# A rank-32 product in four column groups instead of one zero-padded matmul chain

## The chip, the cores and the metric

The kernel runs on one core of one Trainium2 chip. TensorE (PE, with its weight loads PEld), VectorE (DVE), ScalarE (ACT), GpSimd (POOL) and the queue of SyncE (SP) work side by side and wait for each other by semaphores. The metric is the time of one execution on the device in microseconds; a profile of another execution shows where it goes.

## The reference

Windowed attention with eight global keys, then a mixer over the tokens of low rank (32) and a feed-forward part. B = 4 batches, H = 8 heads, S = 768 tokens, D = 64, so 512 channels; U is 768 x 32, V is 32 x 768, w_ch1 is 512 x 2048, w_ch2 is 2048 x 512.

```python
scores = scale * np.matmul(q, k.transpose(0, 1, 3, 2))
...
scores = np.where(keep, scores + bias, -1e9)
a = softmax(scores)
x = np.matmul(a, v)            # (B, H, S, D), then (B, S, H * D)
...
xt = x.transpose(0, 2, 1)
h = xt @ U @ V
u = x + h.transpose(0, 2, 1)
ch = np.maximum(u @ w_ch1, 0.0) @ w_ch2
return u + ch
```

## The kernel before

**Tiling.** Tokens lie on partitions in NSB = 6 tiles of P = 128. Heads go in pairs (NP = 4 pairs a batch), so one step of the outer loop, `i`, is one pair of one batch: 16 steps. A pair is 128 channels, the chunk `dc`. Scores are made transposed, only for the diagonal and the next block of each key tile (`st_SE`, `st_S`, L352 and L357); after the exponential (`ep`), the product with v (`st_V`, L407 and L411) leaves 128 tokens x 65 columns in `ob`, the last column being the sum to divide by. DVE divides into `x_sb` (L424), POOL casts that to `x16` (L425).

**The mixer.** `st_M1` (L428 to L437) multiplies with U: six matmuls, one per token tile, add into one PSUM tile `tmp_ps`, with `u16[:, n]` as the weights (128 tokens x 128 columns) and `x16` (128 tokens x 128 channels) as the moving input. Only R = 32 columns of `u16` hold U, the other 96 are zeros from a memset (L178), so 96 rows of the result are zero. DVE copies it to `tmp16` (L437, 128 x 128, fp16). The product with V contracts over all 128 partitions of `tmp16` and `v16w`, of whose rows only the first 32 hold V and the others zeros. It is done by `st_M2` (L444) for batch 0, where also x is added by matmuls with an identity (L449); by L511 for batch 0's second copy at the output; and by `st_M3` (L474) for the other batches, whose result DVE adds to `x_sb` (L479). All matmuls of the kernel are thus full: 128 rows and 128 columns of weights.

**Feed-forward.** `mk_up` (L497) makes a 128 x 384 piece of the hidden layer from four matmuls into `hps`; ACT takes it to `htr` with Relu (L501). `mk_down` (L517) adds sixteen hidden chunks into `cps`, DVE adds x (L523), SP stores it. These pieces are queued by `queue_ff` and let out a few at a time by `fill(n)` between the steps of the attention.

**Order.** The whole program is recorded in an order written out by hand (`tc.manual_schedule()`), so each engine takes its instructions in the order of the calls. For batch 0 `st_M1(i - 2)` stands before `st_V(i - 1, 0)`; the last of the four stands right before its `st_M2`. In the later loop `st_M1(i - 1)` comes after `fill(1)` and before `st_E(i, 0)`, and `fill(2)` stands between it and `st_M3(i - 1)`, which needs its `tmp16`.

**Queues.** SP issues the loads of q, k and v; POOL issues those of U, V (L179, L180) and of the weights (L219, L222), and after U and V its next work is the cast of v (L126). `tmp_ps`, `ups`, `hps` and `tp` share three PSUM buffers (tag `th`).

Of the kernel before, what the change touches and what calls it, by code (L numbers as in the profile page):

```python
# [12 lines left out]
FP16 = mybir.dt.float16  # L13
# [7 lines left out]
def kernel(  # L21
# [13 lines left out]
    nc = tc.nc  # L35
    B, H, S, D = q.shape
    NG = int(n_global)
    NL = int(n_local)
    P = 128
    DM = H * D  # L40
    NSB = S // P
# [3 lines left out]
    R = moe_U.shape[1]  # L45
    NP = H // 2
    NPE = 2 * NP
    qk_scale = 1.0 / math.sqrt(D)
    BIG = -1.0e9


    assert NG <= 32 and NL <= P - 32 and NG + NL <= P and D == 64 and S % P == 0

    slope = [2.0 ** (-8.0 * (h + 1) / H) for h in range(H)]

# [8 lines left out]
    cst = ctx.enter_context(tc.tile_pool(name="cst", bufs=1))  # L64
# [18 lines left out]
    def ps_th(name, dtype=FP32, cols=512):  # L83
        return psum.tile([P, cols], dtype, name=name, tag="th", bufs=3)
# [5 lines left out]
    def load_qk(i):  # L90
        b, h0 = i // NP, 2 * (i % NP)
        got = []
        for src, nm in ((q, "qst"), (k, "kst")):
            st = stp.tile([P, 2, NSB, D], FP32, name=nm, tag=nm, bufs=2)
            if i < NPE:
                nc.sync.dma_start(
# [53 lines left out]
    def warm(n):  # L150
# [19 lines left out]
    qz = [  # L170
        [cst.tile([P, S], FP16, name=f"qz{s}_{hi}") for hi in range(2)] for s in range(2)
    ]
    nc.vector.memset(qz[0][0][D:P], 0.0)
    nc.vector.memset(qz[0][1][0:D], 0.0)
    u16 = cst.tile([P, NSB, P], FP16, name="u16")
    v16w = cst.tile([P, S], FP16, name="v16w")
    for t in (qz[1][0][D:P], qz[1][1][0:D], u16.rearrange("p n c -> p (n c)"), v16w):
        nc.gpsimd.memset(t.bitcast(I32), 0)  # L178
    nc.gpsimd.dma_start(u16[:, :, 0:R], moe_U.rearrange("(c p) r -> p c r", p=P))  # L179
    nc.gpsimd.dma_start(v16w[0:R], moe_V)  # L180
    ident16 = cst.tile([P, P], FP16, name="ident16")
    nc.vector.tensor_copy(ident16, ident)

# [41 lines left out]
    xs, x16s, tmps, uTs = {}, {}, {}, {}  # L225
# [59 lines left out]
    def st_A(i):  # L285
        vt = vts[i]
        vA = vap.tile([P, NSB - 1, 2, D + 1], FP16, name="vA", tag="vA")
        if i < NPE:
            nc.gpsimd.tensor_copy(vA, vt[:, 0:NSB - 1])
# [11 lines left out]
    def st_P(i):  # L301
        nc.vector.tensor_copy(
            vas[i][0:NG, 1:].rearrange("p n h d -> p n (h d)"),
            vts[i][0:NG, 0:1].rearrange("p n h d -> p n (h d)").broadcast_to(
                (NG, NSB - 2, 2 * (D + 1))
            ),
        )
# [3 lines left out]
    def turn(i):  # L311
        stq, stk = cast.pop(i)
        qT = kp.tile([P, NSB, P], FP16, name="qT", tag="qT")
        kT = kp.tile([P, S], FP16, name="kT", tag="kT")
        nc.sync.dma_start_transpose(
            kT.rearrange("d (n p) -> d n p", n=NSB), stk.rearrange("p n h d -> p (n h d)")
        )
        nc.sync.dma_start_transpose(qT, stq.rearrange("p n h d -> p (n h d)"))
        turned[i] = qT
        kts[i] = kT  # L320
# [7 lines left out]
    def st_K(i):  # L328
        kT = kts[i]
        kA = kp.tile([P, NSB - 1, P], FP16, name="kA", tag="kA")  # L330
        nc.vector.tensor_copy(kA.rearrange("d n p -> d (n p)"), kT[:, 0:S - P])
        nc.vector.tensor_copy(
            kA[:, 1:, 0:NG], kT[:, 0:NG].unsqueeze(1).broadcast_to((P, NSB - 2, NG))
        )
        kas[i] = kA
# [53 lines left out]
    def st_S(i, c):  # L389
        for hi in range(2):  # L390
            s_dve(i, hi, s_pe(i, hi, c))

    def st_E(i, hi):
        ep = scp.tile([P, W], FP16, name=f"ep{hi}", tag=f"ep{hi}")
        nc.scalar.activation(  # L395
            ep, sps.pop((i, hi)), AF.Exp, scale=slope[2 * (i % NP) + hi]
        )
        eps[i, hi] = ep

    def st_V(i, hi):  # L400
        b, h = i // NP, 2 * (i % NP) + hi
        ep, vt, vA = eps.pop((i, hi)), vts[i], vas[i]
        obf = ps_cps("ob") if (i, hi) == (NP - 1, 1) else ps_ob()
        ob = obf[:, 0:NSB * (D + 1)].rearrange("p (n d) -> p n d", n=NSB)
        for qi in range(NSB):
            if qi:
                nc.tensor.matmul(  # L407
                    ob[:, qi], ep[:, OF[qi - 1]:OF[qi - 1] + P], vA[:, qi - 1, hi],
                    start=True, stop=False,
                )  # L410
            nc.tensor.matmul(  # L411
                ob[:, qi], ep[:, DG[qi]:DG[qi] + P], vt[:, qi, hi],
                start=(qi == 0), stop=True,
            )
        rcp = vap.tile([P, NSB], FP32, name="rcp", tag="rcp")
        nc.vector.reciprocal(rcp, ob[:, :, D])
        xo = xs[b][:, :, h * D:(h + 1) * D]
        x16 = x16s[b][:, i % NP, :, hi * D:(hi + 1) * D]
        rb = rcp.unsqueeze(2).broadcast_to((P, NSB, D))
        if i == NP - 1:  # L420
            nc.vector.tensor_tensor(x16, ob[:, :, 0:D], rb, ALU.mult)
            later.append((xo, ob[:, :, 0:D], rb))
            return
        nc.vector.tensor_tensor(xo, ob[:, :, 0:D], rb, ALU.mult)  # L424
        nc.gpsimd.tensor_copy(x16, xo)  # L425


    def st_M1(i):  # L428
        b, dc = i // NP, i % NP
        ch = slice(dc * P, (dc + 1) * P)  # L430
        tps = ps_th("tmp_ps")
        for n in range(NSB):
            nc.tensor.matmul(  # L433
                tps[:, 0:P], u16[:, n], x16s[b][:, dc, n],
                start=(n == 0), stop=(n == NSB - 1),
            )
        nc.vector.tensor_copy(tmps[b][:, ch], tps[:, 0:P])  # L437

# [147 lines left out]
    for i in range(NP):  # L586
        st_SE(i, 0)
        cast_v(i)
        st_A(i)
        if i < 2:  # L590
            load_v(i + 2)
        if i in (1, 2):
            load_qk(NP - 1 + i)
        if i == 2:
            load_w1(0, 2)
        if i == 3:
            load_v(NP)
        if i >= 2:
            st_M1(i - 2)
        if i:  # L600
            st_V(i - 1, 0)
        st_T(i + 1)
        st_SE(i, 1)
        if i:
            st_V(i - 1, 1)
        st_P(i)
        if i >= 2:
            st_M2(i - 2)
        if i < 3:
            cast_qk(i + 2, nc.gpsimd)  # L610
        if i == 3:
            load_w1(2)
            load_w1(3)
        st_SE(i, 2)
    st_M1(NP - 2)
    st_V(NP - 1, 0)
    st_V(NP - 1, 1)
    cast_qk(NP + 1, nc.gpsimd)
    finish_table()
    st_M2(NP - 2)  # L620
    first = [s_pe(NP, hi, 0) for hi in range(2)]
    st_M1(NP - 1)
    st_M2(NP - 1)
    for xo, o, rb in later:
# [6 lines left out]
    for i in range(NP, NPAIR + 2):  # L631
        b, hp = divmod(i, NP)
        live = i < NPAIR
        n = 1 if i < 2 * NP + 1 else 2
# [14 lines left out]
        if NP < i <= NPAIR:  # L649
            st_V(i - 1, 0)  # L650
        if i + 1 < NPE:
            st_T(i + 1)
# [20 lines left out]
        if live:  # L673
            st_S(i, 2)
            if i < NPE:
                st_P(i)
        if i + 1 < NPAIR:
            if i + 1 >= NPE:
                st_K(i + 1)
# [15 lines left out]
        if live:  # L695
            st_E(i, 1)
        if i + 2 < NPAIR and i + 2 >= NPE:
            turn(i + 2)
# [39 lines left out]
```

## Time and profile before

| What | Value |
|---|---|
| Median of 3 runs | 246.03 us (245.66 to 247.09) |
| Profiled execution, first to last instruction | 243.4 us |
| POOL: memset of u16, of v16w | 0.41 us each, at 3.77 and 4.13 us |
| POOL: issue of the load of U, of V | 1.00 and 0.53 us, at 4.49 and 5.48 us |
| U and V, from issue to landing | 6.1 and 5.4 us |
| L433, first and last start | 17.6 and 182.4 us |

The profile gives starts and lengths in microseconds from the first instruction. A line names the source line, the engine, the operation, the tiles as output<-inputs and their sizes; `128*128` is the part of the array that a matmul uses. Matmuls overlap in the pipeline, and their ends are modelled, so the time that a matmul costs the stream is read from start to start. Idle time stands in brackets with what ended it.

### The profile page before, as it was taken

To read this page: it belongs to the slowest core of one execution; us is meant where nothing else is said; L and a number is where in the kernel's file an instruction comes from. 1 tells how busy PE (TensorE), PEld (TensorE's weight loads), DVE (VectorE), ACT (ScalarE), POOL (GpSimd) and SP (SyncE) were. 2 spreads that over 40 slices of the span, in tenths; PEclk is the share of its full clock that TensorE was granted. 3 is DMA by queue.
4 is the path that set the end of the run, shared out by engine and by line. 5 is a ranking of instruction groups with operands and counts; after the bars stand their busy time and mean duration, and the time that the engine had idled before them with its cause. 6 is when DMAs were issued, how large, how long until landed. Compare 5 with 4: busy or idle time off the path is not lost.

```text
span 243.4 us, 4881 instructions
## 1 busy us (share of the span) xinstructions
PE 230.9 (95%) x1952; PEld 141.7 (58%) x1952; DVE 132.4 (54%) x273; ACT 118.8 (49%) x203; POOL 92.8 (38%) x140
## 2 busy tenths in 40 slices
PE   7899879989999999999999999999999999999994
PEld 2577755656565556675656555666565455555453
DVE  7768964868676967675757666755432111011121
ACT  5898648775822211866462507483733134543300
POOL 8379828474464535453544436332111000000000
PEclk9999999999999999999999999999999999999999
DMA  6999999999387999895958682722121200110022
GB/s 195 319 292 298 223 240 274 198 228 225 83 183 176 210 241 166 239 189 136 213 149 196 167 209 80 166 70 57 46 78 32 87 13 34 43 43 34 12 86 86
DMA packets 86030, 36.61 MB, mean 150 GB/s; under 512 B 74136, under 2 KB 82552, under 8 KB 86008
## 3 DMA queue, kind: packets, MB, share of 16 engines
q1 hardware_dynamic: 81480, 32.01, 52.0%
q0 software_dynamic: 4528, 4.29, 10.9%
q8 instruction: 15, 0.25, 0.4%
q14 instruction: 7, 0.06, 0.1%
HBM read 27.46 MB, written 6.29 MB: 139 GB/s over the span
## 4 chain that ended last, share of the span: by engine, by line
PE 75%; DMA 8%; ACT 6%; DVE 5%; POOL 2%; issue 2%; SPq 0%; POOLq 0%
PE cps L517 33%; PE hps L497 29%; DMA w<-in_moe_w_ch_dram 5%; ACT ep L395 3%; PE sc L352 3%; ACT htr L501 3%; DMA vst<-in_v_dram 2%; PE sc L357 2%; PE ob L411 2%; PE cps L535 1%; PE ob L407 1%; PE tmp_ps L433 1%; DVE sp L383 1%; PE ups L474 1%; DVE qz L282 1%
## 5 line engine op out<-in xcount | busy, mean ns | idle before, releaser
L501 ACT ACTIVATE htr<-hps 128x384 f16<-128x384 f32 x128 | 61.7, 491 | 89.6 <-PE hps L497 88.5
L497 PE MATMUL hps<-uT,w 128*128 128x384 f16 x512 | 97.9, 326 | 2.2 <-DMA w<-in_moe_w_ch_dram 1.0
L517 PE MATMUL cps<-w,htr 128*128 128x512 f16 x368 | 90.7, 379 | 0.0
L497 PEld LDWEIGHTS <-w 128*128 128x128 f16 x512 | 47.8, 98 | 33.7 <-issue 2.3
L383 DVE SCALAR_TENSOR_TENSOR sp<-sc,relcat 128x512 f32<-128x512 f32 (+1 forms) x72 | 43.1, 640 | 26.5 <-PE sc L357 21.6
L517 PEld LDWEIGHTS <-htr 128*128 128x128 f16 x368 | 34.6, 98 | 32.6
L523 DVE TENSOR_TENSOR osb<-cps,x_sb 128x512 f32<-128x512 f32 x23 | 15.9, 690 | 51.2 <-PE cps L517 50.9
L395 ACT ACTIVATE ep<-sp 128x1408 f16<-128x1408 f32 x24 | 32.7, 1372 | 12.4 <-DVE sp L383 12.4
L425 POOL CAST x<-x_sb 128x384 f16<-128x384 f32 x30 | 15.4, 513 | 60.4 <-DVE x_sb L424 60.4
L352 PE MATMUL sc<-qz,kT 128*128 128x128 f16 x192 | 27.6, 219 | 0.5 <-DVE sp L383 0.5
L357 PE MATMUL sc<-qz,kA 128*128 128x128 f16 x160 | 25.3, 219 | 0.2 <-DVE kA L276 0.2
L352 PEld LDWEIGHTS <-kT 128*128 128x128 f16 x192 | 18.3, 98 | 4.2 <-DVE kT L261 0.4
L357 PEld LDWEIGHTS <-kA 128*128 128x128 f16 x160 | 15.6, 98 | 6.8 <-issue 0.8
L482 POOL CAST x<-x_sb 128x768 f16<-128x768 f32 x12 | 9.9, 829 | 20.5 <-DVE x_sb L479 20.5
L424 DVE TENSOR_TENSOR x_sb<-ob,rcp 128x384 f32<-128x384 f32 x30 | 16.7, 557 | 1.0
L479 DVE TENSOR_TENSOR x_sb<-ups,x_sb 128x384 f32<-128x384 f32 x24 | 12.3, 552 | 7.7 <-PE ups L474 7.6
L411 PE MATMUL ob<-v,ep 128*128 128x65 f16 x192 | 15.8, 193 | 0.0
L126 POOL CAST v<-vst 128x768 f16<-128x768 f32 x16 | 13.4, 840 | 4.6 <-DMA vst<-in_v_dram 4.6
L411 PEld LDWEIGHTS <-ep 128*128 128x128 f16 x192 | 13.9, 98 | 2.1
L407 PE MATMUL ob<-vA,ep 128*128 128x65 f16 x160 | 13.9, 194 | 0.0
L326 POOL COPY qz<-qT 64x768 f16<-64x768 f16 x16 | 13.4, 836 | 0.7 <-DMA qT<-q 0.2
L407 PEld LDWEIGHTS <-ep 128*128 128x128 f16 x160 | 10.9, 97 | 2.1
(79 smaller groups left out, 196.7 us busy)
## 6 DMA issues: line engine op xcount, KB each, us to landing
qst<-in_q_dram SPq DMA_DIRECT2D x16, 384.0 KB, 5.4
kst<-in_k_dram SPq DMA_DIRECT2D x16, 384.0 KB, 5.2
vst<-in_v_dram SPq DMA_DIRECT2D x16, 384.0 KB, 6.3
out_dram<-osb SPq DMA_DIRECT2D x23, 256.0 KB, 2.0
w<-in_moe_w_ch_dram POOLq DMA_DIRECT2D x6, 512.0 KB, 8.7
vA<-v SPq DMA_DIRECT2D x8, 152.3 KB, 3.6
w<-in_moe_w_ch_dram POOLq DMA_DIRECT2D x1, 1024.0 KB, 12.4
out_dram<-osb SPq DMA_DIRECT2D x2, 128.0 KB, 1.7
```

The source lines that it names most:

```text
L352: nc.tensor.matmul(sc[:, o:o + P], kT[:, kb * P:(kb + 1) * P], z[:, kb * P:(kb + 1) * P], start=(o == 0 and not on_pe), stop=(o + P == tot),)
L357: nc.tensor.matmul(sc[:, o + P:o + 2 * P], kA[:, kb], z[:, (kb + 1) * P:(kb + 2) * P], start=False, stop=(o + 2 * P == tot),)
L383: nc.vector.scalar_tensor_tensor(out=sps[i, hi][:, c0:c0 + tot], in0=sc[:, 0:tot], scalar=qk_scale / slope[2 * (i % NP) + hi], in1=relf[:, ...
L395: nc.scalar.activation(ep, sps.pop((i, hi)), AF.Exp, scale=slope[2 * (i % NP) + hi])
L407: nc.tensor.matmul(ob[:, qi], ep[:, OF[qi - 1]:OF[qi - 1] + P], vA[:, qi - 1, hi], start=True, stop=False,)
L411: nc.tensor.matmul(ob[:, qi], ep[:, DG[qi]:DG[qi] + P], vt[:, qi, hi], start=(qi == 0), stop=True,)
L424: nc.vector.tensor_tensor(xo, ob[:, :, 0:D], rb, ALU.mult)
L425: nc.gpsimd.tensor_copy(x16, xo)
L497: nc.tensor.matmul(hps[:, 0:GT], w1_16[:, dc, jt * P:(jt + 1) * P], uT[:, dc, ts], start=(dc == 0), stop=(dc == NDC - 1),)
L501: nc.scalar.activation(cell["htr"][:, jt], hps[:, 0:GT], AF.Relu)
L517: nc.tensor.matmul(cps, htr[:, jc, t * P:(t + 1) * P], w2_16[:, jc], start=(b > 0 and jc == 0), stop=(jc == NJC - 1),)
L523: nc.vector.tensor_tensor(osb, cps, x_sb[:, n], ALU.add)
```

## The change

Each of the six matmuls with U now uses 32 columns of weights and writes to its own group of 32 PSUM partitions: token tile n goes to group g = n % 4, so groups 0 and 1 get two token tiles, groups 2 and 3 one. `tmp_ps` then holds four partial sums one above the other. V is loaded four times, one copy per group of 32 partitions of `v16w`, so that the product with V, which contracts over 128 partitions as before, adds the four partial sums. `u16` shrinks to its 32 columns, and its memset and that of `v16w` go.

```diff
+    NG4 = P // R
...
-    u16 = cst.tile([P, NSB, P], FP16, name="u16")
+    u16 = cst.tile([P, NSB, R], FP16, name="u16")
     v16w = cst.tile([P, S], FP16, name="v16w")
-    for t in (qz[1][0][D:P], qz[1][1][0:D], u16.rearrange("p n c -> p (n c)"), v16w):
+    for t in (qz[1][0][D:P], qz[1][1][0:D]):
         nc.gpsimd.memset(t.bitcast(I32), 0)
-    nc.gpsimd.dma_start(u16[:, :, 0:R], moe_U.rearrange("(c p) r -> p c r", p=P))
-    nc.gpsimd.dma_start(v16w[0:R], moe_V)
+    nc.gpsimd.dma_start(u16, moe_U.rearrange("(c p) r -> p c r", p=P))
+    for g in range(P // R):
+        nc.gpsimd.dma_start(v16w[g * R:(g + 1) * R], moe_V)
...
         for n in range(NSB):
+            g = n % NG4
             nc.tensor.matmul(
-                tps[:, 0:P], u16[:, n], x16s[b][:, dc, n],
-                start=(n == 0), stop=(n == NSB - 1),
+                tps[g * R:(g + 1) * R, 0:P], u16[:, n], x16s[b][:, dc, n],
+                start=(n < NG4), stop=(n + NG4 >= NSB),
             )
```

The order of the instructions on every engine stays as it was, but for the two memsets and the three loads on POOL. The first weight load with `tmp16` waits for all loads of V, and three of the later loads of weights on POOL wait for loads of U and V that were issued long before.

More of the change, by code (lines that the diff above doesn't have):

```diff
@@ L52 @@
     assert NG <= 32 and NL <= P - 32 and NG + NL <= P and D == 64 and S % P == 0
+    assert R == 32
     slope = [2.0 ** (-8.0 * (h + 1) / H) for h in range(H)]
```

## The prediction

> **What bounds the kernel now.** I read the page first, then a table of stretches, then PE's waits, then the matmuls around the edited product one by one. One profiled execution is the base: 243.4 us from first to last instruction. The median of the runs shown is 246.03, so 2.6 us lie around the span; every term below is added to both alike.
>
> ```profile
> PE 230.9 (95%) x1952; PEld 141.7 (58%) x1952; DVE 132.4 (54%) x273; ACT 118.8 (49%) x203; POOL 92.8 (38%) x140
> ...
> PEclk9999999999999999999999999999999999999999
> ```
>
> PE is busy 95% at a full granted clock. That average hides three stages, which the table of stretches separates (after the stretch and its length: PE, PEld, DVE, ACT and POOL busy, then clock, DMA share and GB/s).
>
> ```profile
> 0.00:33.10 33.10, 27.53 (x334) 19.23 (x334) 25.23 (x67) 24.54 (x47) 23.71 (x42) 1.00 1.04 267
> 33.10:64.00 30.90, 28.50 (x276) 19.40 (x277) 21.81 (x41) 22.49 (x38) 17.88 (x27) 1.00 1.15 219
> 64.00:184.50 120.50, 119.27 (x1038) 73.08 (x1036) 77.32 (x155) 54.55 (x84) 50.39 (x70) 1.00 0.63 151
> ```
>
> Up to 33.1 the DMA engines are full (share 1.04) and PE has gaps; from 64 to 184.5 PE is busy 119.27 of 120.50, and anything that PE does longer there makes the kernel longer. PE's waits from 64 us to the end are only these:
>
> ```profile
> PE ups L474 <- DVE tmp L437: 0.6, 2, 0.4
> PE ups L474 <- ACT htr L501: 0.4, 1, 0.4
> ```
>
> The early stage ends on a transfer: in the chain that ended last stand a load of v and then the first w_ch1 load, for which PE waits.
>
> ```profile
> 8.04 6.04 DMA vst<-in_v_dram
> ...
> 20.65 12.43 DMA w<-in_moe_w_ch_dram
> ```
>
> ```profile
> 33.13 0.34 PE L497 MATMUL hps<-uT,w 128*128 128x384 f16 x1 [1.03 <-DMA w<-in_moe_w_ch_dram]
> ```
>
> **The product with U, and what a switch can cost.** L433 runs 16 times with six matmuls each. Its matmuls (least, median and greatest ns), then, from the timeline of PE, one of its turns in the full stream (start us, length us, engine, line, operation):
>
> ```profile
> L433 PE MATMUL tmp_ps<-x,u x96: 216/219/219, 17.6 to 182.4; 128*128 128x128 f16 x96
> ```
>
> ```profile
> 132.85 0.81 PE L497 MATMUL hps<-uT,w 128*128 128x384 f16 x4
> 133.50 0.50 PE L433 MATMUL tmp_ps<-x,u 128*128 128x128 f16 x6
> 133.84 0.38 PE L517 MATMUL cps<-w,htr 128*128 128x512 f16 x1
> ```
>
> A matmul lasts 219 ns in the records, but six span 0.50 us: five steps of (498 - 219) / 5 = 56 ns. From 133.50 to the next product at 133.84 is 0.34 us = 6 x 56. That is all that this product costs PE: 16 x 0.334 = 5.3 us. The difference of 219 - 56 = 163 ns is the tail of a matmul that the next one overlaps (for the 384-column form it is 326 less its step of 162, again about 163).
>
> The edit makes each of these a 128 x 32 tile of the array instead of a full one; every other matmul of the program stays 128*128. So PE changes its tile shape 32 times, where before it never did. No row shows a matmul on part of the columns or a change of shape. I bound three pieces.
>
> (a) *Inside the six.* Highest: they keep the 56 ns step, gain nothing. Lowest: the four groups run fully together, so that only one full step lies between the first four and the last two, 4 x 56 = 222 ns gained. The nearest row is the quickest pace at which the trace shows PE starting matmuls, the 65-column ones:
>
> ```profile
> 18.00 0.20 PE L407 MATMUL ob<-vA,ep 128*128 128x65 f16 x1
> 18.04 0.19 PE L411 MATMUL ob<-v,ep 128*128 128x65 f16 x1
> 18.07 0.19 PE L407 MATMUL ob<-vA,ep 128*128 128x65 f16 x1
> ```
>
> About 28 ns a start with one weight load each. I take that pace: 5 x (56 - 28) = 140, rounded down to 138 ns gained.
>
> (b) *Each switch.* Lowest: 0, the stream goes on. Highest: the whole tail is waited for and then a whole weight load of 98 ns (the length of every PEld row of L433) lies open: 163 + 98 = 261 ns. What an open load costs, one row shows: a load that waits with its matmul.
>
> ```profile
> 12.80 0.10 PEld L357 LDWEIGHTS <-kA 128*128 128x128 f16 x1 [0.32 <-DVE kA L276]
> 12.80 0.23 PE L357 MATMUL sc<-qz,kA 128*128 128x128 f16 x1 [0.15 <-DVE kA L276]
> 12.82 0.10 PEld L347 LDWEIGHTS <-slI 128*128 128x128 bf16 x1
> 12.87 0.38 PE L347 MATMUL sc<-rel,slI 128*128 128x512 bf16 x1
> ```
>
> The next start comes 70 ns after, not 56: 14 ns. I take the full tail plus this, 163 + 14 = 177 ns, on the reading that the array is not given another shape while a matmul is in it. [...]
>
> (c) *A full-stream turn:* two switches less the gain, 2 x 177 - 138 = +216 ns (bounds: -222, and 2 x 261 = +522).
>
> **Where it lands.** The 16 turns fall into four groups.
> - Turns 1 to 4 (17.6 to 30.4 us): PE waits 1.03 us at 33.13 for the w_ch1 load, whose issue at 20.65 depends on no turn but for what precedes turn 1. They cost 0; without that cover they would cost 0.04 to 0.2 us each, 0.5 us at most.
> - Turns 5 and 6 (50.11, 61.34): PE stands idle before them (0.54 us for ACT, 0.29 us for POOL), so the entry is free: 177 - 138 = +39 ns each, 0.08 us.
> - Turns at 96.66, 108.47 and 158.61: within 2 us after them PE waits for tmp of DVE or htr of ACT (the rows above, 0.6 + 0.4 us, besides the tail). DVE reaches tmp late because of its copies to kA ahead of it, not because of the product, so 0 each; with the cover gone 216 each, 0.65 us.
> - The other seven, from 71.88 to 182.14: 7 x 0.216 = +1.51 us.
>
> PE together: +1.59 us.
>
> The rest of the edit: DVE's copy of tmp stays 128 x 128, the product with V has the same shapes, PE does the same count of instructions. On POOL two memsets of 0.41 us go and three more loads of V come at 0.53 us of issue each: +0.77 us, in the 4.13 us for which POOL then waits for v:
>
> ```profile
> 10.14 0.83 POOL L126 CAST v<-vst 128x768 f16<-128x768 f32 x1 [4.13 <-DMA vst<-in_v_dram]
> ```
>
> Behind them in POOL's queue stands that cast; were the cover gone, it would be 0.77 us late and the w_ch1 issue with it. The first product with V comes at 20.8 us and the landing of V was at 10.9 (issued at 5.48, 5.4 us to landing), so its wait for four loads is free, as are the waits on these loads that the changed program puts before w_ch issues after 20.65.
>
> But the transfers themselves are not free. The page's queue of POOL's loads:
>
> ```profile
> q0 software_dynamic: 4528, 4.29, 10.9%
> ```
>
> 10.9% of 243.4 us is 26.5 us of all 16 engines for 4.29 MB, thus 0.30 us for one load of V (48.0 KB in the list of DMA issues) and 0.9 us for three. DMA is full there, and v's landing at 14.08 leads the chain to 33.13. Bounds 0 (gaps between packets take it) and 0.9; a gain is excluded, since nothing on that chain waits for the memsets. I take the middle, 0.5 us.
>
> Sum: 1.59 + 0.5 = +2.1 us: span 245.5, **time 248.1 us** (+0.9%). Its own range: least, switches of 163 ns and the 222 ns gain, 7 x 0.104 - 2 x 0.06 + 0 = +0.6 (246.6); most, switches of 261 with 138 gained, 7 x 0.384 + 2 x 0.123 + 0.9 = +3.8 (249.8).
>
> [...]
>
> **The rivals.**
> 1. *The groups overlap and the switches cost nothing* (faster). Each full-stream turn gains 222 ns: 7 x 0.222 + 2 x 0.222 = 2.0 us, less 0.5 for V: 244.5; 244.0 if the loads are hidden. For it: four separate column groups with four separate inputs need nothing of each other. Against: a load and a matmul of another shape would have to run beside a tail of 163 ns. It decides below 2 x 69 ns of switch per turn, where the 138 ns are not yet eaten. 0.2.
> 2. *The groups do not overlap and the switches are short, or the two cancel* (the change does not do what it says). PE +0, V +0.5: 246.5. For it: the pace of 28 ns is of short inputs, and 128 columns took 56 everywhere. 0.15.
> 3. *No overlap, and each switch costs a tail and a whole load* (slower still): 7 x 0.522 + 2 x 0.261 = 4.2, plus 0.9: 251.1. Turns with cover stay covered (522 ns against waits of about as much). Against: the one open load seen cost 14 ns, not 98. 0.15.
>
> **How the numbers follow.** The forecast gets 0.5, the rivals 0.2, 0.15 and 0.15. About 0.5% (1.2 us, so 244.8 and 247.3) is what the runs can tell from no change. Faster: rival 1, 0.2. Same: rival 2 and the lower part of the forecast's range, 0.15 + 0.1 = 0.25. Slower: 0.4 + 0.15 = 0.55. The range runs from just under rival 1 with its loads half hidden, 244.2, to rival 3, 251.0; about 0.1 is left out on each side.
>
> **What will show it.** In the changed profile, at a full-stream turn: the first of the six starts about 177 ns later after the 384- or 512-column step than before (162 or 216 ns), the six starts lie about 28 ns apart, the next matmul starts some 233 ns after the last instead of 56. Starts within a few ns and no gaps at the ends: rival 1. Steps of 56: rival 2 or 3. For V: the cast of v at 14.13 and the hps start at 33.13 move by up to 0.9 us. I am wrong if the six wait for each other, group by group: five tails of 163 more per turn would be some 9 us in all.

## The result and the profile after

The changed kernel takes 247.55 us (median of 17 runs, 245.56 to 251.22) against 245.66 us for the kernel before (17 runs): ratio 1.0081, 95% interval 1.0060 to 1.0103, so about 2.0 us slower. The ratio leaves out the runs that lie over 1.5% above the fastest of their kernel. The profiled execution is 246.0 us from first to last instruction, 2.6 us above that of before.

The page of the changed kernel, busy time by engine:

```profile
PE 230.0 (94%) x1952; PEld 137.3 (56%) x1952; DVE 132.7 (54%) x273; ACT 118.9 (48%) x203; POOL 94.1 (38%) x141
```

PE is 0.9 us *less* busy than before (230.9), although the kernel is longer. The table of stretches, cut at the first hps, 2.6 us later than before (columns as before: PE, PEld, DVE, ACT, POOL busy, clock, DMA share, GB/s):

```profile
0.00:35.70 35.70, 27.02 (x334) 18.28 (x334) 27.33 (x69) 24.72 (x47) 24.81 (x43) 1.00 1.05 254
35.70:66.50 30.80, 28.36 (x276) 18.98 (x277) 20.51 (x38) 22.43 (x38) 17.89 (x27) 1.00 1.23 218
66.50:187.00 120.50, 118.91 (x1037) 70.02 (x1035) 76.78 (x154) 54.59 (x84) 50.61 (x70) 1.00 0.71 151
```

The first stretch holds the same 334 matmuls as before in 2.6 us more, and the third, where PE is the bound, holds the same work but for one matmul record (1037, before 1038) in the same 120.5 us. The chain that ended last and PE's wait at the first hps say where the 2.6 us are:

```profile
8.03 7.98 DMA vst<-in_v_dram
...
22.15 13.56 DMA w<-in_moe_w_ch_dram
```

```profile
35.75 0.50 PE L501 MATMUL hps<-uT,w 128*128 128x384 f16 x2 [2.45 <-DMA w<-in_moe_w_ch_dram]
```

v's second load lands at 16.01 instead of 14.08, the w_ch1 load is issued at 22.15 instead of 20.65 and lands 2.6 us later, and PE waits 2.45 us instead of 1.03. From the first hps to the end both profiles take the same: 243.36 - 33.13 = 210.2 and 245.96 - 35.75 = 210.2 us.

POOL's timeline shows where the delay begins (start, length, line, operation):

```profile
3.78 1.25 POOL L181 DMA_DIRECT2D u<-in_moe_U_dram  x1
5.03 2.06 POOL L183 DMA_DIRECT2D v16w<-in_moe_V_dram  x4
11.29 0.83 POOL L128 CAST v<-vst 128x768 f16<-128x768 f32 x1 [4.21 <-DMA vst<-in_v_dram]
```

The issues of the loads are hidden: POOL waits 4.21 us for v behind them all the same (4.13 before). But v itself comes later: its cast starts at 11.29 instead of 10.14.

The turn of the product with U that was shown of before, now in PE's timeline of the changed kernel:

```profile
135.56 0.81 PE L501 MATMUL hps<-uT,w 128*128 128x384 f16 x4
136.31 0.29 PE L437 MATMUL tmp_ps<-x,u 128*32 128x128 f16 x6
136.53 0.82 PE L521 MATMUL cps<-w,htr 128*128 128x512 f16 x3
```

From the hps group to the first of the six: 0.75 us, before 0.65. The six records now span 0.29 us instead of 0.50. From the first of the six to the next product: 0.22 instead of 0.34. So the turn costs PE 0.97 us where it cost 0.99. By the single starts the entry is 256 ns after the last hps instead of 162 (+94), the six start 3, 4, 3, 57 and 3 ns apart (70 ns instead of 278), the next product starts 152 ns after the last instead of 56 (+96), and the step behind it is 11 ns longer. Sum: -7 ns a turn.

One more thing moved, in the stall behind a covered turn. PE's waits from 66 us to the end:

```profile
PE ups L478 <- ACT htr L505: 0.9, 2, 0.4
PE hps L501 <- DVE x_sb L483: 0.4, 1, 0.4
PE ups L478 <- DVE tmp L441: 0.3, 1, 0.3
```

A wait of hps for DVE's x_sb has appeared that the kernel before does not have there.

### The profile page after: what moved, and what is told of

Read it like the earlier page. It is cut to its first block, busy times and chain, and to the rows that moved or that the text cites. A ratio compares the mean times of both kernels' runs of the same rounds, so it can differ in the third digit from the quotient of the medians.

```text
span 246.0 us, 4882 instructions
## 1 busy us (share of the span) xinstructions
PE 230.0 (94%) x1952; PEld 137.3 (56%) x1952; DVE 132.7 (54%) x273; ACT 118.9 (48%) x203; POOL 94.1 (38%) x141
## 4 chain that ended last, share of the span: by engine, by line
PE 74%; DMA 9%; DVE 7%; ACT 5%; POOL 2%; issue 2%; SPq 0%; POOLq 0%; DVEq 0%
PE cps L521 32%; PE hps L501 29%; DMA w<-in_moe_w_ch_dram 6%; DMA vst<-in_v_dram 3%; PE sc L355 3%; ACT ep L398 2%; PE sc L360 2%; ACT htr L505 2%; PE ob L414 2%; DVE sp L386 1%; PE cps L539 1%; PE ups L478 1%; PE ob L410 1%; DVE qz L285 1%; PE tmp_ps L437 1%
```

## The experiments

Ratios are against runs of the kernel before on the same chip, with 95% intervals.

**V loaded once, three copies on chip.** The column groups and the early issue stay.

```diff
-    for g in range(P // R):
-        nc.gpsimd.dma_start(v16w[g * R:(g + 1) * R], moe_V)
+    nc.gpsimd.dma_start(v16w[0:R], moe_V)
...
         st_P(i)
+        if i == 1:
+            nc.vector.tensor_copy(v16w[R:2 * R], v16w[0:R])
+            nc.scalar.copy(v16w[2 * R:3 * R], v16w[0:R])
+            nc.vector.tensor_copy(v16w[3 * R:4 * R], v16w[0:R])
```

> The column groups stay, V is loaded once, and its three other copies are made on chip (two copies by DVE, one by ACT, at i = 1). Theory 1 (the loss is the three extra loads of V, which hold back v's second load and so the w_ch1 load; the column groups cost PE nothing, about -8 ns a turn): the time comes back to that of the kernel before, ratio 0.998 to 1.003; v's second load lands near 14.1 us again, the first hps starts near 33.1. Theory 2 (the loss is PE's 32 changes of tile shape, as forecast +1.6 us): ratio about 1.006, and v lands early all the same.

Measured: 1.0044 (1.0014 to 1.0074). By the medians about half of the loss went, 0.0037 of 0.0081. The interval reaches into the first theory's range (up to 1.003) and holds the second's 1.006, so this run alone does not decide between them. The profiled execution had its first hps at 33.48 us and a span of 243.3, but the spans of the twelve runs go from 243.3 to 245.9 us: one profile shows one of these. v's second load alone is issued at 8.04 us in the profile of before and at 8.48, 8.45 and 8.56 in those of the column groups alone, of the four switches and of the other order below, where the edit changes nothing ahead of it. So the readings below rest on the ratios, and on what many profiles show alike.

**More loads of V, and nothing else.** The kernel before with three, then six more loads into memory that the w_ch2 load overwrites later.

```diff
+    vmore = w2_16[:, 0:2].rearrange("p a b -> p (a b)")
+    for g in range(1, P // R):
+        nc.gpsimd.dma_start(vmore[g * R:(g + 1) * R, 0:S], moe_V)
```

> The kernel before, full 128-column product with U, with three more loads of V into memory that is overwritten later, issued behind the load of V. Theory 1: as slow as the changed kernel, ratio about 1.008 (+2.0 us), v's second load lands near 16.0 us, the first hps starts near 35.7. Theory 2: at most the 0.5 us of the forecast, ratio 1.002.

> The kernel before with six more loads of V instead of the three of e2; the product with U stays full. If each load holds back the early stage by its 0.3 us: twice e2, ratio 1.006 to 1.009, first hps 1.5 to 2 us later than before. If e2 was noise: 0.999 to 1.003.

Measured: three loads 1.0037 (0.9999 to 1.0075), six loads 1.0077 (1.0050 to 1.0105). Twice the dose, twice the loss: 0.9 and 1.9 us, 0.3 us a load. The interval of the three still reaches 0, that of the six goes from 1.2 to 2.6 us, 0.2 to 0.4 us a load. Neither kernel has a column group, and V loaded once, which takes three loads out of the changed kernel, wins, by the medians, the same 0.0037 that three loads cost here. The chain, first with three loads, then with six:

```profile
8.35 6.85 DMA vst<-in_v_dram
21.77 12.46 DMA w<-in_moe_w_ch_dram
```

```profile
8.21 7.63 DMA vst<-in_v_dram
22.43 12.37 DMA w<-in_moe_w_ch_dram
```

v's second load lands at 15.20 and 15.84 (before 14.08), the w_ch1 issue slips to 21.77 and 22.43 (20.65), and the first hps starts at 34.28 and 34.84. From there to the end they take 210.2 and 210.3 us, as before (210.2).

**The hour of the loads.** Kernel before, the loads of U and V ahead of the memsets of the unused parts, or behind memsets done three times; and the change with two memsets ahead of its loads.

```diff
-    for t in (qz[1][0][D:P], qz[1][1][0:D], u16.rearrange("p n c -> p (n c)"), v16w):
+    for t in (qz[1][0][D:P], qz[1][1][0:D]):
...
+    for t in (u16[:, :, R:], v16w[R:2 * R], v16w[2 * R:]):
+        nc.gpsimd.memset(t.bitcast(I32), 0)
```

> The kernel before with the memsets of the unused parts of u16 and v16w behind the loads of U and V, so that these are issued 0.8 us earlier, as in the changed kernel; no load is added. If the earlier issue, not the number of loads, holds back v: slower by a good part of 2 us, ratio 1.004 or more. Theory 1: no change, ratio 0.998 to 1.002.

> The kernel before with the memsets of u16 and v16w done three times, so that U and V are issued 1.6 us later (near 6.1 and 7.1 us) in POOL's idle time. If the hour of U's and V's transfers decides how long v is held back: the other way than e3, ratio 0.994 to 0.998. If not: 0.999 to 1.002.

> The changed kernel with two memsets of 0.41 us kept ahead of the loads, so that U and V are issued at 4.5 us as before; the three more loads of V stay. If number and hour of the loads each hold back the early stage by about 0.35%: ratio about 1.004 to 1.006. If only the number counts: 1.008, as the change.

Measured: earlier 1.0035 (0.9996 to 1.0074), later 0.9996 (0.9968 to 1.0023), the change at the old hour 1.0107 (1.0051 to 1.0164). Inconclusive: the first allows a cost of the earlier hour, the third wins nothing back by undoing it, and its interval holds the change's own 1.0081. The edits also met the hours only in part. In POOL's timelines the first moves the issue of U from 4.49 to 3.78 us, but V's stays at 5.50 (5.48 before), because U's issue grew from 1.00 to 1.72 us; the second has them at 5.93 and 7.33; the third has U at 4.92 and V from 6.25 us, later than before. And three of the third's six runs have a mean granted clock of 0.993 or less, which goes with a stretch at half clock (told at the end); the other three took 246.6 to 247.9 us. That the hour matters is neither shown nor excluded.

**The extra loads of V later.**

```diff
         st_A(i)
+        if i == 0:
+            for g in range(1, P // R):
+                nc.gpsimd.dma_start(v16w[g * R:(g + 1) * R], moe_V)
```

> The changed kernel with its three extra loads of V issued by POOL behind the first cast of v (near 12 us instead of 5.5 to 7.1). If the loss is that v's second load is held back: most of it is won back, ratio 1.000 to 1.004 against the kernel before, v's second load lands within 0.5 us of 14.1. If the loss is bytes on DMA engines that are full until 60 us, wherever they stand: still 1.008, and the first hps starts near 35.7 again.

Measured: 1.0096 (1.0058 to 1.0133); nothing won back. But the edit has a cost of its own, seen in POOL's timeline: the three issues now stand between the copy of vA and the casts of q and k, and in the chain that ended last. So it does not tell what a later hour alone would do.

```profile
12.49 0.73 POOL L291 COPY vA<-v 128x650 f16<-128x650 f16 x1
13.17 1.46 POOL L595 DMA_DIRECT2D v16w<-in_moe_V_dram  x3
14.62 0.84 POOL L114 CAST q<-qst 128x768 f16<-128x768 f32 x1
```

**U and V by SP's queue, behind v's second load, cast on chip**, with the full product and with the column groups.

```diff
     load_v(1)
+    nc.sync.dma_start(ust, moe_U.rearrange("(c p) r -> p c r", p=P))
+    nc.sync.dma_start(vwst[0:R], moe_V)
     load_qk(3)
```

> The kernel before with U and V loaded in fp32 by SP's queue behind v's second load, and cast on chip (DVE, ACT) at i = 1; nothing of theirs then runs beside the first loads of q, k and v. If the collision with U and V sets the early stage: v's second load lands 0.5 to 1 us earlier (13.1 to 13.6), ratio 0.994 to 0.998. If it only moves the bytes behind: 1.000, or slower where the product with U waits for U.

> The column groups of the changed kernel, with U and V loaded once each by SP behind v's second load and V cast four times on chip. By the theory the best of both: the gain of e7 plus 0.1 us, ratio 0.993 to 0.998. By the rival that the shape changes cost: about 0.006 above e7.

Measured: 1.0085 (1.0052 to 1.0119) and 1.0117 (1.0073 to 1.0161). Both were to be faster; neither is. In the profile with the full product v's second cast did start earlier, at 13.41 instead of 14.13, but the load of w_ch1 was issued 0.65 us later, took longer (12.43 before), and the first hps started at 35.23.

```profile
21.30 13.88 DMA w<-in_moe_w_ch_dram
```

That the bytes were only moved behind v fits the longer load; no run shows it by itself. A part of both ratios is the half clock told at the end: seven of the ten runs and four of the six have a mean clock of 0.993 or less, and the other three with the full product took 246.1 to 246.6 us.

**The column groups alone.** u16, v16w, memsets and the two loads stand as before; V is copied on chip.

```diff
+            g = n % 4
             nc.tensor.matmul(
-                tps[:, 0:P], u16[:, n], x16s[b][:, dc, n],
-                start=(n == 0), stop=(n == NSB - 1),
+                tps[g * R:(g + 1) * R, 0:P], u16[:, n, 0:R], x16s[b][:, dc, n],
+                start=(n < 4), stop=(n + 4 >= NSB),
```

> The kernel before with the column groups alone: u16, v16w, their memsets and the two loads stand as before, so DMA and POOL start as before; V's three copies are made on chip at i = 1 (DVE two, ACT one). Theory now (PE's changes of tile shape cost about what the groups save; the loss is in the early transfers, part from the loads issued earlier, part from three more): ratio 0.998 to 1.002, time from the first hps to the end 210.0 us (before 210.2). If the column groups themselves cost something that the profiles of single runs hid: 1.004 or more.

Measured: 1.0012 (0.9983 to 1.0041). The groups neither save nor cost anything that can be told. Of the versions with column groups this is the one nearest to the kernel before; none beats it.

**Twice as many changes of tile shape.** A full matmul of zeros after the fourth and sixth of the six.

```diff
+            if n in (3, 5):
+                nc.tensor.matmul(
+                    tps[:, 0:P], zw[:, 0:P], zw[:, 0:P], start=False, stop=(n == 5)
+                )
```

> e5 with a full 128*128 matmul of zeros (it adds nothing) after the fourth and after the sixth of the matmuls with U, so that each turn changes the tile shape four times instead of twice. If a switch costs the 95 ns that the starts show: about 0.30 us more a turn than e5, of which 0.11 is the two matmuls; seven uncovered turns make 2.1 us, ratio about 1.010. If the gaps are only in the records and nothing waits: 0.8 us, ratio about 1.004.

Measured: 1.0108 (1.0070 to 1.0147), as the priced switch had it. The turn in PE's timeline:

```profile
135.53 0.24 PE L434 MATMUL tmp_ps<-x,u 128*32 128x128 f16 x4
135.70 0.23 PE L439 MATMUL tmp_ps<-zw 128*128 128x128 f16 x1
135.86 0.23 PE L434 MATMUL tmp_ps<-x,u 128*32 128x128 f16 x2
136.03 0.23 PE L439 MATMUL tmp_ps<-zw 128*128 128x128 f16 x1
136.09 0.38 PE L522 MATMUL cps<-w,htr 128*128 128x512 f16 x1
```

Each change of shape takes 0.16 to 0.17 us from start to start where a full matmul takes 0.06. From the start of turn 5 to that of turn 7, two turns, this kernel takes 22.33 us and the groups alone 21.71: 0.31 us a turn. The gaps are time that PE loses, not a way of recording.

**Neighbours of one group.** Token tiles in the order 0, 4, 1, 5, 2, 3.

```diff
-        for n in range(NSB):
+        for n in (0, 4, 1, 5, 2, 3):
```

> e5 with the token tiles in the order 0, 4, 1, 5, 2, 3, so that matmuls of one column group follow each other. If two matmuls of one group follow at the full step of 56 ns and those of different groups at 3 to 4 ns, a full-stream turn shows steps near 56, 3, 56, 3, 3 (120 ns and more instead of 70). If groups overlap with anything: 70 ns again.

Measured: one run, 246.72 us beside a median of 245.25 of the kernel before; the groups alone ran from 244.78 to 248.57, so the two are not to be told apart in time. The starts lie 7, 6, 4, 49 and 6 ns apart, 72 ns in all.

```profile
134.95 0.29 PE L434 MATMUL tmp_ps<-x,u 128*32 128x128 f16 x6
135.18 0.61 PE L518 MATMUL cps<-w,htr 128*128 128x512 f16 x2
```

The order changes nothing: four records start within some 17 ns whichever group they belong to, the fifth starts about 50 ns behind the fourth, and the next product starts 0.23 us after the first, as in the order 0 to 5. With the second of the six on the first's group and still 7 ns behind it, a start in the record is no sign that the matmul has the group to itself.

## Why the prediction was right, and which steps were not

The forecast was +2.1 us; +2.0 came. Direction and size hold, but the terms of its sum do not: 1.59 of the 2.1 us were to come from the changes of tile shape, which cost PE next to nothing. That dearer loads and about 1.1 us from elsewhere filled the gap is luck.

*The switch* was mis-sized. Forecast 177 ns each, the whole tail of 163 plus 14; measured 94 on entry and 96 on exit, the step behind the exit 11 more, the same within 2 ns at all seven uncovered turns. So a change of shape adds less than the tail of 163: the first matmul of the new shape starts some 70 ns before the modelled end of the last of the old one (256 ns after a start that is put at 326 ns long). The 177 ns rested on the reading that the array is not given another shape while a matmul is in it. No run shows that (the ends are modelled), nor a switch of 177 ns; the runs show 94 and 96 ns more from start to start in its place.

*The gain inside the six* was mis-sized too. Forecast 138 ns, from the pace of the 65-column matmuls; measured 208, near its bound of 222. In the turn shown the first four of the six start 3 to 4 ns apart, the fifth 57 ns behind the fourth.

So *a full-stream turn* is -7 ns instead of +216, and the seven uncovered ones give about -0.05 us instead of +1.51. Two errors of the same sign, a switch too dear and a gain too small, made the largest term of the sum wrong. The second rival's way, the two cancel, is what PE did; even the least that the forecast's range gave PE, +0.6 us, was too much.

*The loads of V* were forecast at 0.5 us, the middle between 0 and 0.9. The measured price is the upper end, 0.3 us a load and 0.9 for three: on DMA engines that are full (share 1.05) and lead the chain, no gap is seen to have swallowed them. The step that divided queue 0's time by its bytes had the price right; taking the middle was the error. The sign named for it, that v's second cast and the first hps move by up to 0.9 us, was passed: they moved by 1.9 (14.13 to 16.06) and 2.6 us in the one profile, by 1.1 in that of three loads and nothing else.

*The three covered turns at 0* failed. Behind `st_M3` of these turns (the 9th, 10th and 14th) the next hps waits for DVE's add of x_sb where it waited for ACT; the semaphore that the instruction waits for is another. That it gets another of the three buffers of tag `th` is a reading, as no view names the buffers. In PE's timeline of the profile before and of the changed kernel:

```profile
110.56 0.63 PE L474 MATMUL ups<-tmp,v16w 128*128 128x128 f16 x6 [0.29 <-DVE tmp L437]
111.24 0.48 PE L497 MATMUL hps<-uT,w 128*128 128x384 f16 x2
```

```profile
112.92 0.62 PE L478 MATMUL ups<-tmp,v16w 128*128 128x128 f16 x6 [0.30 <-DVE tmp L441]
113.97 0.81 PE L501 MATMUL hps<-uT,w 128*128 128x384 f16 x4 [0.42 <-DVE x_sb L483]
```

0.68 us from ups to hps became 1.05. The stretch from turn 9 to turn 11, which holds two of the three turns, takes 24.69 to 24.70 us in all six profiles of kernels with the full product, and 24.62 to 25.63 us in seven with groups, the changed kernel's being 24.97. The eighth, the one with four switches, got the old wait for ACT back behind these turns and takes 24.69, although each of its turns is some 0.3 us longer: there the cover holds, as the prediction counted on. V loaded once has the new wait and yet takes 24.62; in the two turns of that stretch its ups wait for ACT first (0.8 us in both together), and by then DVE is done. That speaks for the wait and against the groups themselves; no run changed the wait alone.

What makes up the 2.0 us, then: about 0.9 for three loads is shown by dose. The rest, about 1.1, is not settled. The new waits (from nothing to 0.9 us in the profiles) fit in it, but in the changed kernel's own profile they lengthen that stretch by 0.3 and the time from the first hps to the end not at all. The earlier hour of the loads is neither shown nor excluded, and the groups alone may cost up to 1.0 us by their interval. The half clock told below makes little of it. One stretch of 3.4 us at one half takes 1.7 of some 246 us from a run's clock, so its mean is 0.993. Of the changed kernel's 17 runs 7 show 0.993 or less, of the 79 of the kernel before that stand beside the experiments 8. But the changed kernel's ten other runs have a median of 247.1 us, still 1.8 to 2.0 above the medians of the others there (245.1 to 245.3, measured at other hours).

## What to carry to other kernels

The matmuls narrowed to pack column groups paid here for two changes of tile shape: 0.20 us a turn, as much as the six gained by running together (0.21), so by these figures the packed stretch must be longer than that or share its switches. Copies that a layout needs are not free because their issue is: in a stage led by full DMA engines (share 1.05 here), price them at their whole transfer time, 0.3 us a load of V. After an edit of a tile's shape, compare what its neighbours wait for, even if no instruction moved. And when a sum comes out right, compare its terms too: here the largest measured nothing.

## What had not been expected of the hardware

A wait of PE for data was followed by a stretch at half clock: in the profile of the column groups alone 1.33 us of waiting by 3.4 us of it. The first hps group behind the wait there, and the stretches around it (last three columns: clock, DMA share, GB/s):

```profile
33.83 2.47 PE L498 MATMUL hps<-uT,w 128*128 128x384 f16 x8 [1.33 <-DMA w<-in_moe_w_ch_dram]
```

```profile
30.00:34.00 4.00, 2.15 (x29) 1.37 (x27) 2.98 (x8) 1.34 (x3) 2.52 (x5) 1.00 1.14 278
34.00:38.00 4.00, 4.00 (x24) 2.67 (x23) 1.27 (x3) 1.93 (x4) 0.00 (x0) 0.57 1.22 203
38.00:42.00 4.00, 4.00 (x35) 2.68 (x34) 3.47 (x6) 2.94 (x6) 3.24 (x6) 1.00 1.02 268
```

The eight matmuls take 2.47 us; in the profile of before they took 1.48:

```profile
33.13 1.48 PE L497 MATMUL hps<-uT,w 128*128 128x384 f16 x8 [1.03 <-DMA w<-in_moe_w_ch_dram]
```

That the clock is a half shows in the profile of U and V by SP's queue with the full product: 0.50 from 34 to 38 us. So a clock of 0.57 over 4 us is 3.4 us at one half, and the way from the first hps to turn 5 is 18.27 us instead of 16.98, 1.3 us lost. Four of the fourteen profiles have this at the first hps, with waits of 1.1 to 2.5 us there, and others with waits as long, the changed kernel's 2.45 us among them, do not. Taken at one half, the clock from 34 to 42 us makes this 3.4 us long in three of the four (0.57 and 1.00; 0.77 and 0.80 for U and V by SP's queue with the column groups; 0.69 and 0.88 for the change at the old hour) and 6.8 us in the fourth (0.50 and 0.65), where it is there at 34 us and PE waits until 35.23. Two more have it earlier: V's extra loads later and U and V later show 0.94 over the first 30 us and 1.00 from there to 42. What decides it no run shows.
